# Seven block products whose banks alternate, and a new instruction order from the second token group on

## The chip, the core and the metric

The kernel runs on one core of one Trainium2 chip. The metric is the device time of one execution in microseconds (us): the median of three runs of the kernel before is 733.15 us (731.96 to 734.58).

Engine names as in the profile: PE is TensorE's matmul stream, PEld its weight loads, DVE VectorE, ACT ScalarE, POOL GpSimd, SP SyncE (which issues most of the DMAs). Each engine works through its own list of instructions in order and waits where an operand is not ready.

## The reference

An attention over 768 tokens of four sequences (eight heads of 64), with a local window and block summaries, feeds a gated feed-forward layer over all 3072 tokens:

```python
k_sum = k.reshape(B, H, nb, 32, D).max(axis=3)
v_sum = v.reshape(B, H, nb, 32, D).mean(axis=3)
scores_l = scale * q @ k.T            # kept where |i - j| < 16
scores_s = scale * q @ k_sum.T + log(32)
a = softmax(concat([scores_l, scores_s]))
attn = a @ concat([v, v_sum])
...
x = attn as (3072, 512)
xn = x / sqrt(mean(x * x) + 1e-6) * rms_g
g, val = xn @ w_gate, xn @ w_val      # 512 -> 1536
out = (silu(g) * val) @ w_out         # 1536 -> 512
```

Every product is made of 16-bit halves: a value is split into a high and a low part, and three matmuls (high by high, high by low, low by high) stand for one.

## The kernel before

**Units and groups.** Attention is done in 24 units of 128 tokens. For unit u: `prep_k` and `prep_q` scale, split and transpose (by a DMA) keys and queries, `scores u g` makes the scores of four heads, `expo u g` the exponentials, which a DMA transposes into `eT`, `attend u` multiplies them with the values that `prep_v` has put into `v1`, `v2h` and `v2l`, and `norm_a`, `norm_b` normalise the result and transpose it by a DMA into the group's `xT`. `v2h` exists once for all units: `prep_v` of the next unit writes half of it on ACT (L757), a DMA issued by POOL (L758) copies that half to the other partitions, and neither may start before the last `attend` that reads the old content.

The feed-forward layer takes the tokens in nine groups (384, 128, 256, then six of 384). Groups 0 to 4 use `gate_val grp f` (L1177: 12 matmuls for the gate, 12 for the value of 128 features, one PSUM bank each, two banks of the name `gv` in turn; then a tanh on ACT at L1181, two DVE operations at L1182 and L1184, and the split into `hh` on ACT and `hl` on DVE). `project grp f` (L1207) multiplies `hh` and `hl` with the output weights, three matmuls for each 128 tokens.

**Seven products.** Half the features of group 5 and all of groups 6 to 8 use a scheme with seven block products in place of eight. `make_t` prepares sums of the weights, `make_s grp c` (POOL, ACT, DVE) sums of the tokens, `seven grp f2` the seven products of two times 256 features, and `swish` what follows. A product is 12 matmuls of 192 columns (L1113). `seven` has two PSUM banks. Called X and Y here (Z is the bank of Y, used before it), they are filled in the program in this order, where X accumulates over four products and is copied out by ACT after each:

| product | X1 | Z2 | X3 | Y4 | X5 | X6 | Y7 |
|---|---|---|---|---|---|---|---|
| read out by | ACT L1135 | DVE L1138 | ACT L1140 | with X5 | ACT L1144, then DVE L1145 adds Y | ACT L1147 | DVE L1149 |

A product into a bank that is being read out waits for the reader.

**Who sets the order.** `PLAN` is a list of 764 steps in the order in which the program is recorded. `ORDER` then gives, engine by engine, a permutation of the recorded instructions (as jumps and run lengths), and `in_order` chains each engine's instructions to it. So products of one `seven` stand between matmuls of `project`, `scores` and `attend`, and may be exchanged where the data allow it.

Of the kernel before, what the change touches and what calls it, by code (L numbers as in the profile page):

```python
# [82 lines left out]
project 2 1 256 512; conv_o 0; sum_fold 2 0 0 2; gate_val 2 3 256; fill_k 10; expo 7 1; sum_load 2 0 0 3;
scores 8 0; project 2 2 256 512; scores 8 1; gate_val 2 4 256; sum_fold 2 0 0 3; project 2 3 256 512; conv_o 1;
prep_q 9; expo 8 0; gate_val 2 5 256; sum_load 2 0 1 0; attend 7; fill_k 11; project 2 4 256 512; prep_v 8;
gate_val 2 6 256; sum_load 2 0 1 1; load_unit 11; project 2 5 256 512; conv_o 2; expo 8 1; gate_val 2 7 256;
attend 8; gate_val 2 8 256; norm_a 7; project 2 6 256 512; sum_fold 2 0 1 0; sum_fold 2 0 1 1;
project 2 7 256 512; conv_o 3; gate_val 2 9 256; norm_b 7; scores 9 0; sum_load 2 0 1 2; prep_v 9;
gate_val 2 10 256; sum_fold 2 0 1 2; scores 9 1; norm_a 8; project 2 8 256 512; sum_load 2 0 1 3; norm_b 8;
project 2 9 256 512; conv_o 4; sum_fold 2 0 1 3; load_ks 2; gate_val 2 11 256; prep_q 10; expo 9 0;  # L90
sum_scale 2 0; project 2 10 256 512; gate_val 3 0 384; sum_load 2 1 0 0; gate_val 3 1 384; sum_fold 2 1 0 0;
sum_load 2 1 0 1; project 2 11 256 512; conv_o 5; expo 9 1; gate_val 3 2 384; scores 10 0; sum_fold 2 1 0 1;
split_ks 2; sum_load 2 1 0 2; load_k 12; project 3 0 384 768; sum_fold 2 1 0 2; gate_val 3 3 384;
sum_load 2 1 0 3; expo 10 0; attend 9; prep_k 12; project 3 1 384 768; prep_v 10; gate_val 3 4 384;
sum_fold 2 1 0 3; load_k 13; scores 10 1; sum_load 2 1 1 0; prep_k 13; fill_k 12; norm_a 9; expo 10 1;
project 3 2 384 768; project 3 3 384 768; norm_b 9; gate_val 3 5 384; sum_load 2 1 1 1; prep_q 11;
sum_fold 2 1 1 0; sum_fold 2 1 1 1; load_k 15; prep_k 14; fill_k 13; gate_val 3 6 384; sum_load 2 1 1 2;
sum_fold 2 1 1 2; project 3 4 384 768; load_k 16; sum_load 2 1 1 3; scores 11 0; project 3 5 384 768;
gate_val 3 7 384; expo 11 0; sum_fold 2 1 1 3; load_unit 12; load_unit 13; sum_load 3 0 0 0; attend 10;
prep_v 11; scores 11 1; gate_val 3 8 384; norm_a 10; prep_q 12; project 3 6 384 768; sum_scale 2 1; norm_b 10;  # L100
sum_load 3 0 0 1; expo 11 1; gate_val 3 9 384; prep_k 15; fill_k 14; project 3 7 384 768; attend 11; load_k 17;
prep_v 12; gate_val 3 10 384; load_unit 14; norm_a 11; prep_q 13; project 3 8 384 768; sum_fold 3 0 0 0;
sum_fold 3 0 0 1; sum_load 3 0 0 2; norm_b 11; prep_q 14; project 3 9 384 768; load_unit 15; sum_fold 3 0 0 2;
scores 12 0; scores 12 1; gate_val 3 11 384; expo 12 0; project 3 10 384 768; sum_load 3 0 0 3;
gate_val 4 0 384; prep_k 16; fill_k 15; sum_fold 3 0 0 3; expo 12 1; load_k 18; sum_load 3 0 1 0;
gate_val 4 1 384; make_t 0; make_t 1; load_unit 16; scores 13 0; project 3 11 384 768; sum_load 3 0 1 1;
gate_val 4 2 384; project 4 0 384 1152; project 4 1 384 1152; scores 13 1; gate_val 4 3 384; make_t 2;
make_t 3; expo 13 0; attend 12; project 4 2 384 1152; prep_k 17; fill_k 16; gate_val 4 4 384; prep_v 13;
expo 13 1; project 4 3 384 1152; gate_val 4 5 384; make_t 4; make_t 5; norm_a 12; prep_q 15; scores 14 0;
attend 13; project 4 4 384 1152; gate_val 4 6 384; norm_b 12; load_unit 17; expo 14 0; prep_v 14;  # L110
gate_val 4 7 384; project 4 5 384 1152; scores 14 1; norm_a 13; gate_val 4 8 384; sum_fold 3 0 1 0;
sum_fold 3 0 1 1; expo 14 1; sum_load 3 0 1 2; fill_k 17; project 4 6 384 1152; sum_fold 3 0 1 2;
gate_val 4 9 384; prep_q 16; norm_b 13; sum_load 3 0 1 3; project 4 7 384 1152; attend 14; scores 15 0;
sum_fold 3 0 1 3; load_ks 3; gate_val 4 10 384; sum_load 3 1 0 0; prep_v 15; project 4 8 384 1152;
sum_load 3 1 0 1; norm_a 14; sum_scale 3 0; sum_fold 3 1 0 0; sum_fold 3 1 0 1; expo 15 0;
project 4 9 384 1152; split_ks 3; scores 15 1; sum_load 3 1 0 2; gate_val 4 11 384; norm_b 14; load_k 19;
project 4 10 384 1152; sum_fold 3 1 0 2; sum_load 3 1 0 3; prep_k 18; sum_fold 3 1 0 3; project 4 11 384 1152;
prep_q 17; load_k 20; expo 15 1; gate_val 5 6 384; sum_load 3 1 1 0; prep_k 19; fill_k 18; gate_val 5 7 384;
make_t 6; make_t 7; load_k 21; sum_fold 3 1 1 0; project 5 6 384 1536; gate_val 5 8 384; scores 16 0;
attend 15; project 5 7 384 1536; sum_load 3 1 1 1; gate_val 5 9 384; make_t 8; expo 16 0; sum_fold 3 1 1 1;  # L120
scores 16 1; sum_load 3 1 1 2; prep_v 16; gate_val 5 10 384; sum_fold 3 1 1 2; norm_a 15; project 5 8 384 1536;
expo 16 1; norm_b 15; prep_k 20; fill_k 19; gate_val 5 11 384; make_s 5 0; make_s 5 1; make_t 9;
sum_load 3 1 1 3; scores 17 0; seven 5 0; sum_fold 3 1 1 3; load_unit 18; load_unit 19; project 5 9 384 1536;
load_k 22; sum_scale 3 1; attend 16; expo 17 0; prep_v 17; project 5 10 384 1536; norm_a 16; prep_q 18;
norm_b 16; seven 5 1; swish 5 0 1; load_unit 20; project 5 11 384 1536; make_t 10; swish 5 0 0; scores 17 1;
project 5 0 384 1536; expo 17 1; project 5 1 384 1536; make_t 11; swish 5 1 1; seven 5 2; swish 5 1 0;
scores 18 0; prep_k 21; fill_k 20; load_k 23; attend 17; expo 18 0; prep_v 18; norm_a 17; prep_q 19; norm_b 17;
swish 5 2 1; project 5 2 384 1536; prep_q 20; swish 5 2 0; load_unit 21; make_s 6 0; scores 18 1;
project 5 3 384 1536; make_s 6 1; seven 6 0; project 5 4 384 1536; project 5 5 384 1536; expo 18 1; prep_k 22;
fill_k 21; load_unit 22; swish 6 0 1; seven 6 1; swish 6 0 0; scores 19 0; expo 19 0; attend 18;  # L130
project 6 0 384 1920; prep_v 19; project 6 1 384 1920; swish 6 1 1; seven 6 2; swish 6 1 0; norm_a 18;
prep_q 21; norm_b 18; swish 6 2 1; project 6 2 384 1920; swish 6 2 0; seven 6 3; scores 19 1;
project 6 3 384 1920; expo 19 1; project 6 4 384 1920; prep_k 23; fill_k 22; scores 20 0; load_unit 23;
attend 19; swish 6 3 1; expo 20 0; seven 6 4; prep_v 20; project 6 5 384 1920; swish 6 3 0; norm_a 19;
scores 20 1; prep_q 22; project 6 6 384 1920; expo 20 1; fill_k 23; norm_b 19; swish 6 4 1; swish 6 4 0;
scores 21 0; seven 6 5; project 6 7 384 1920; attend 20; project 6 8 384 1920; prep_v 21; norm_a 20; prep_q 23;
norm_b 20; expo 21 0; project 6 9 384 1920; swish 6 5 1; swish 6 5 0; scores 21 1; make_s 7 0; make_s 7 1;
seven 7 0; project 6 10 384 1920; project 6 11 384 1920; expo 21 1; swish 7 0 1; seven 7 1; swish 7 0 0;
scores 22 0; project 7 0 384 2304; attend 21; expo 22 0; swish 7 1 1; seven 7 2; project 7 1 384 2304;
swish 7 1 0; prep_v 22; scores 22 1; project 7 2 384 2304; project 7 3 384 2304; swish 7 2 1; seven 7 3;  # L140
expo 22 1; norm_a 21; norm_b 21; swish 7 2 0; scores 23 0; attend 22; expo 23 0; seven 7 4; swish 7 3 1;
prep_v 23; swish 7 3 0; norm_a 22; scores 23 1; project 7 4 384 2304; norm_b 22; project 7 5 384 2304;
# [1115 lines left out]
```

## Time and profile before

| | |
|---|---|
| median of three runs | 733.15 us (731.96 to 734.58) |
| profiled execution, its own time | 731.4 us |
| its span, first to last instruction | 729.4 us |
| PE busy | 684.8 us, 94% of the span, 5846 matmuls |
| DVE busy | 587.9 us, 81% |
| ACT busy | 478.1 us, 66% |
| POOL busy | 314.5 us, 43% |
| granted TensorE clock, mean | 0.992 |

A matmul's duration in the trace is longer than the distance to the next one, because they are pipelined: work is read from start to start. Idle time in square brackets is the time that an engine stood still before a row, and the name behind it what ended that.

### The profile page before, as it was taken

Reading aid. Unit: us, or ns where it says so; the run is one execution under the profiler, and the core shown is the slowest. Engines: PE = TensorE matmul, PEld = TensorE weight load, DVE = VectorE, ACT = ScalarE, POOL = GpSimd, SP = SyncE. Lnnn points to the kernel's source line nnn. Section 1 sums busy time; section 2 is a strip of 40 time slices with the busy share of each in tenths; the row PEclk is TensorE's granted clock in tenths of the full one; section 3 lists DMA queues with packets and bytes.
Section 4 is the critical chain, followed back from the end, with each engine's and each line's share of the span. In section 5 each row is a group of like instructions: output and inputs, shape, how many; then the busy total and the mean of one; then the engine's idle time right before and its main releaser. Section 6 shows DMA issues by size and latency. Waiting matters only on the chain.

```text
span 729.4 us, 16150 instructions
## 1 busy us (share of the span) xinstructions
PE 684.8 (94%) x5846; PEld 495.2 (68%) x5846; DVE 587.9 (81%) x1594; ACT 478.1 (66%) x1023; POOL 314.5 (43%) x421
## 2 busy tenths in 40 slices
...
GB/s 196 310 306 247 204 98 112 112 112 125 153 153 139 117 106 184 178 141 172 131 110 133 114 182 113 123 148 117 91 106 118 113 91 71 48 53 44 2 1 44
DMA packets 243860, 93.33 MB, mean 128 GB/s; under 512 B 227716, under 2 KB 227716, under 8 KB 243780
## 3 DMA queue, kind: packets, MB, share of 16 engines
...
q0 software_dynamic: 1152, 1.22, 0.7%
q8 instruction: 46, 0.75, 0.5%
...
## 4 chain that ended last, share of the span: by engine, by line
PE 50%; DVE 16%; DMA 11%; ACT 9%; issue 6%; POOL 5%; SPq 1%; ACTq 0%; DVEq 0%; POOLq 0%
PE gv L1113 14%; PE acc L1207 14%; PE gv L1177 13%; ACT sm L791 2%; DMA eT<-ee 2%; PE att L948 2%; PE att L817 2%; DVE hl L372 2%; DMA hn<-in_v_dram 1%; PE att L776 1%; DVE sm L780 1%; DMA hn<-in_k_dram 1%; DVE w L474 1%; DVE v2l L759 1%; DVE th L1184 1%
## 5 line engine op out<-in xcount | busy, mean ns | idle before, releaser
L1177 PE MATMUL gv<-xT,w_gv 128*128 128x384 f16 (+2 forms) x1584 | 228.7, 299 | 10.9 <-DVE th L1182 9.3
L1177 PEld LDWEIGHTS <-w_gv 128*128 128x128 f16 x1584 | 141.5, 98 | 89.5 <-issue 22.6
L1207 PE MATMUL acc<-wo,hh 128*128 128x512 f16 (+1 forms) x576 | 178.0, 391 | 1.0 <-ACT hh L1164 0.7
L372 POOL TENSOR_TENSOR ee<-sm,ee 128x512 f16<-128x512 f32 (+1 forms) x72 | 72.2, 1018 | 104.0 <-ACT ee L367 99.4
L1207 PE MATMUL acc<-wo,hl 128*128 128x512 f16 (+1 forms) x288 | 110.8, 385 | 5.3 <-DVE hl L372 4.5
L1113 PEld LDWEIGHTS <-w_gv 128*128 128x128 f16 x1008 | 84.3, 98 | 11.5 <-issue 5.0
L791 ACT ACTIVATE sm<-sm,mx,c 128x192 f32<-128x192 f32 x144 | 68.9, 537 | 14.1 <-DVE mx L783 13.3
L1207 PEld LDWEIGHTS <-hh 128*128 128x128 f16 x432 | 39.8, 98 | 31.3 <-ACT hh L1164 1.1
L1181 ACT ACTIVATE th<-gv,gains 128x384 f32<-128x384 f32 (+2 forms) x66 | 33.9, 514 | 27.6 <-PE gv L1177 21.9
L1113 PE MATMUL gv<-S,w_gv 128*128 128x192 f16 x504 | 48.4, 246 | 3.0 <-ACT R L1144 1.9
L1113 PEld LDWEIGHTS <-wo 128*128 128x128 f16 x540 | 45.4, 98 | 5.7 <-issue 2.1
L372 DVE TENSOR_TENSOR hl<-th,hh 128x384 f16<-128x384 f32 (+3 forms) x66 | 44.0, 671 | 5.7 <-ACT hh L367 5.4
L780 DVE CUSTOM_DVE_ANT_0 sm<-att,mask 128x192 f32<-128x192 f32 x144 | 45.1, 349 | 3.2 <-PE att L776 1.7
L1113 PE MATMUL gv<-xT,w_gv 128*128 128x192 f16 x504 | 47.3, 246 | 0.3 <-ACT R L1147 0.3
L367 ACT CAST hh<-th 128x384 f16<-128x384 f32 (+3 forms) x66 | 29.3, 447 | 22.7 <-DVE th L1184 15.1
L1182 DVE SCALAR_TENSOR_TENSOR th<-th,gv 128x384 f32<-128x384 f32 (+2 forms) x66 | 31.2, 473 | 12.9 <-ACT th L1181 12.6
L1207 PEld LDWEIGHTS <-hl 128*128 128x128 f16 x216 | 21.1, 98 | 29.7 <-DVE hl L372 2.9
L618 ACT ACTIVATE junk<-hn 96x512 uint8<-96x512 f32 x48 | 30.0, 626 | 13.4 <-DMA hn<-in_v_dram 9.2
L367 ACT CAST ee<-sm 128x512 f16<-128x512 f32 (+1 forms) x72 | 34.2, 508 | 2.8 <-DMA eT<-ee 1.9
L758 POOL DMA_DIRECT2D v2h<-v2h x36 | 19.7, 548 | 36.9 <-ACT v2h L757 35.5
L1010 POOL TENSOR_TENSOR x_r<-x_r,consts 128x1 f32<-128x1 f32 x24 | 17.3, 721 | 42.0 <-DVE x_r L1009 41.5
L1113 PE MATMUL gv<-xT,wo 128*128 128x192 f16 x360 | 34.8, 246 | 0.5 <-DVE xT L1101 0.5
...
## 6 DMA issues: line engine op xcount, KB each, us to landing
...
```

Source lines behind the costliest of these rows:

```text
L367: nc.scalar.copy(o, i)
L372: (nc.vector if ENG.get(op, "p") == "v" else nc.gpsimd).tensor_tensor(o, a, b, op=ALU.subtract)
L618: nc.scalar.activation(junk[0:96], y[:, o:o + DM], AF.Square, accum_out=d["ss"][:, j:j + 1])
L758: {"s": nc.sync, "a": nc.scalar, "p": nc.gpsimd}[ENG.get("v2q", "a")].dma_start(v2h[other, r], v2h[rs, r])
L780: nc.vector.tensor_tensor_reduce(sm[:, i, :], pt[:, j * SC:(j + 1) * SC], mask, 1.0, NEG, op0=ALU.add, op1=ALU.max, accum_out=mx[:, i:i + 1])
L791: nc.scalar.activation(sm[:, i, :], sm[:, i, :], AF.Exp, scale=s["c"][:, 0:1], bias=mx[:, i:i + 1])
L1010: nc.gpsimd.tensor_tensor(r, r, nhalf, op=ALU.pow)
L1113: nc.tensor.matmul(bank[:, i * T2:(i + 1) * T2], lhsT=right(n, wi, c), rhs=left(xi, c), start=start, stop=(i == 1 and c == 1 and wi == 1), ...
L1177: nc.tensor.matmul(pt[:, 0:T], lhsT=w_gv[:, f - f % 2 + i, wi, c, f % 2, :], rhs=x[:, xi, c, 0:T], start=(n == 0), stop=(n == 3 * NC - 1))
L1181: nc.scalar.activation(th[:, 0:T], pg[:, 0:T], AF.Tanh, scale=f_sc[:, f - f % 2:f - f % 2 + 1])
L1182: nc.vector.scalar_tensor_tensor(th[:, 0:T], th[:, 0:T], 1.0, pg[:, 0:T], op0=ALU.add, op1=ALU.mult)
L1207: nc.tensor.matmul(accs[grp][j], lhsT=h[:, js], rhs=wo_hl[f // 2][:, wi, f % 2, :], start=(f == first and n == 0), stop=(f == (first - 1) ...
```

## The change

Two things change, and no instruction is added or removed: PE has 5846 matmuls in both.

First, in `seven`, Y4 and not X5 becomes the product that is copied out by ACT, X5 is added to it by DVE, and Y7 goes ahead of X6:

```diff
             product(Y, lambda xi, c: x[:, xi, c, up], tee(2), True)
+            nc.scalar.copy(r[1][:, :, 1], half(Y))
             product(X, ess(2), tee(0))
-            nc.scalar.copy(r[1][:, :, 1], half(X))
-            nc.vector.tensor_tensor(r[1][:, :, 1], r[1][:, :, 1], half(Y), op=ALU.add)
+            nc.vector.tensor_tensor(r[1][:, :, 1], r[1][:, :, 1], half(X), op=ALU.add)
+            product(Y, lambda xi, c: x[:, xi, 2 + c, up], tee(3))
+            nc.vector.tensor_tensor(r[0][:, :, 1], r[0][:, :, 1], half(Y), op=ALU.add)
             product(X, ess(1), block(1, 1))
             nc.scalar.copy(r[1][:, :, 0], half(X))
-            product(Y, lambda xi, c: x[:, xi, 2 + c, up], tee(3))
-            nc.vector.tensor_tensor(r[0][:, :, 1], r[0][:, :, 1], half(Y), op=ALU.add)
```

Second, `PLAN` from its 270th step on and `ORDER` of all five engines are new. PE's list is the same for its first 856 of 5701 recorded matmuls, which is up to 153.9 us of the trace of before. One line of each table:

```diff
-project 0 11 384 0; load_unit 9; load_unit 10; prep_k 10; fill_k 9; gate_val 2 0 256; project 1 10 128 384;
...
+gate_val 2 0 256; sum_load 2 0 0 2; project 2 0 256 512; gate_val 2 1 256; sum_fold 2 0 0 0; scores 7 1;
...
--39x12 27x3 -30x24 -124x10 246x9 -129x12 -138x18 120x45 259x3 -322x3 57x21 241x6 -247x12 24x3 211x3 -241x24 18 198x3
...
+-39x12 27x3 -30x24 -124x10 246x9 -129x12 -138x18 120x45 259x3 -322x3 57x21 244x3 -247x12 24x3 -27x12 217x3 -190 192x3
...
```

The new tables are four lines longer, so the code behind them has numbers higher by four in the lists of the kernel after (L791 is L795, L372 is L376). In `seven` the line numbers after are L1139 (copy of X1), L1144 (X3), L1147 (Y4), L1149 (adds X5), L1151 (adds Y7) and L1153 (copy of X6).

ACT, at the products of `seven 6 0` and the start of `seven 6 1` (`gv_7469` is X of `seven 6 0` before; after, `gv_7478` is its X, `gv_7519` its Y and `gv_7611` the X of `seven 6 1`). Before:

```order
L791 ACTIVATE sm_7429<-sm_7429,mx_7430,c_6912 128x192 x3
L1140 COPY R_7467<-gv_7469 128x2x192
L367 CAST ee_7590<-sm_7429 128x2x2x64
L1217 DMA out_0_dram<-ob_7587 128x512
L367 CAST ee_7590<-sm_7429 128x4x128
L1144 COPY R_7468<-gv_7469 128x2x192
L733 ACTIVATE qs_7392<-qr_l_7030,q_s_7384 128x8x64
L1147 COPY R_7468<-gv_7469 128x2x192
```

After:

```order
L1147 COPY R_7477<-gv_7519 128x2x192
L795 ACTIVATE sm_7414<-sm_7414,mx_7415,c_6924 128x192 x2
L1144 COPY R_7476<-gv_7478 128x2x192
L1221 DMA out_0_dram<-ob_7575 128x512
L371 CAST ee_7598<-sm_7414 128x2x2x64
L1221 DMA out_0_dram<-ob_7581 128x512
L371 CAST ee_7598<-sm_7414 128x4x128
L737 ACTIVATE qs_7407<-qr_l_7074,q_s_7399 128x8x64
L1139 COPY R_7609<-gv_7611 128x2x192
L1153 COPY R_7477<-gv_7478 128x2x192
```

Before, three copies in a row read the same bank X; now the copies of Y, X, the next `seven`'s X, and X follow each other.

ACT, at `prep_v 8` (L757 writes the two halves of `v2h` for unit 8, L761 its `v1`; L1181 is a gate's tanh, L791 the exponentials of `expo 8 1`, L592 the weights of `conv_o`). Before:

```order
L757 ACTIVATE v2h_142<-v2r_l_2689,kv1_s_2160 64x4x64
L1181 ACTIVATE th_3387<-gv_3361,gains_129 128x256
L761 ACTIVATE v1h_140<-vr_l_2688,kv1_s_2160 128x8x64
L757 ACTIVATE v2h_142<-v2r_l_2689,kv1_s_2160 64x4x64
L791 ACTIVATE sm_3154<-sm_3154,mx_3155,c_2836 128x192 x4
```

After:

```order
L761 ACTIVATE v2h_142<-v2r_l_2689,kv1_s_2160 64x4x64
L596 ACTIVATE wo1_3380<-cv_3376,scales_2135 128x512
L596 ACTIVATE wo1_3380<-cv_3378,scales_2135 128x512
L761 ACTIVATE v2h_142<-v2r_l_2689,kv1_s_2160 64x4x64
L1185 ACTIVATE th_3282<-gv_3256,gains_129 128x256
L371 CAST hh_3252<-th_3248 128x256
L765 ACTIVATE v1h_140<-vr_l_2688,kv1_s_2160 128x8x64
```

The second half of `v2h` now stands ahead of `v1h`, a tanh and a split of `gate_val`, where it stood behind them.

POOL, at the normalisation of unit 17, the last of group 6 (L1010 is `norm_a`, `xs` the split of `norm_b` that the transposing DMA into `xT` waits for, `ee` the splits of `expo 18 0`). Before:

```order
L758 DMA v2h_142<-v2h_142 64x264 x2
L1010 TENSOR_TENSOR x_r_7336<-x_r_7336,consts_86 128x1
L372 TENSOR_TENSOR ee_7314<-sm_7236,ee_7314 128x2x128
L372 TENSOR_TENSOR xs_7359<-x_7263,xs_7359 128x512
L372 TENSOR_TENSOR ee_7314<-sm_7236,ee_7314 128x4x128
```

After:

```order
L762 DMA v2h_142<-v2h_142 64x264 x2
L1014 TENSOR_TENSOR x_r_7336<-x_r_7336,consts_86 128x1
L376 TENSOR_TENSOR xs_7340<-x_7263,xs_7340 128x512
L376 TENSOR_TENSOR ee_7322<-sm_7244,ee_7322 128x2x128
L376 TENSOR_TENSOR ee_7322<-sm_7244,ee_7322 128x4x128
```

`xs` of unit 17 moved ahead of both splits of the exponentials.

## Rows read from the trace of the kernel before

**Rows 1.** Stages: stretch, length, busy PE, PEld, DVE, ACT, POOL, PE clock, DMA.

```profile
201.60:264.70 63.10, 57.77 (x518) 47.11 (x517) 53.18 (x152) 44.91 (x105) 29.74 (x32) 0.97 0.75 131
...
462.10:655.20 193.10, 186.83 (x1972) 149.82 (x1970) 155.36 (x443) 133.74 (x294) 83.75 (x103) 1.00 0.54 97
```

**Rows 2.** Waits of PE from 201 us on: who for whom, total us, times, longest.

```profile
PE gv L1177 <- DVE th L1182: 4.3, 5, 1.1
PE att L817 <- DMA v2h<-v2h: 2.0, 1, 2.0
PE gv L1113 <- ACT R L1144: 1.9, 3, 0.7
PE att L817 <- DMA eT<-ee: 1.4, 2, 1.2
PE gv L1113 <- ACT R L1140: 1.1, 2, 0.6
PE gv L1177 <- DVE th L1184: 1.0, 1, 1.0
```

**Rows 3.** Timeline of PE at X5, X6, Y7 of seven 6 0, and at X5, X6 of 8 0.

```profile
514.52 1.15 PE L1113 MATMUL gv<-S,w_gv 128*128 128x192 f16 x12 [0.57 <-ACT R L1140]
516.24 1.15 PE L1113 MATMUL gv<-S,w_gv 128*128 128x192 f16 x12 [0.57 <-ACT R L1144]
517.23 1.15 PE L1113 MATMUL gv<-xT,wo 128*128 128x192 f16 x12
...
663.13 1.15 PE L1113 MATMUL gv<-S,w_gv 128*128 128x192 f16 x12
665.00 1.15 PE L1113 MATMUL gv<-S,w_gv 128*128 128x192 f16 x12 [0.72 <-ACT R L1144]
```

**Rows 4.** Timeline around attend 7 and attend 8, all engines.

```profile
234.76 0.19 PE L817 MATMUL att<-v2h,eT 128*128 128x65 f16 x1
...
234.79 4.09 PE L1177 MATMUL gv<-xT,w_gv 128*128 128x256 f16 x36
...
236.48 0.52 POOL L758 DMA_DIRECT2D v2h<-v2h  x1 [3.20 <-ACT v2h L757]
...
241.88 0.20 PE L817 MATMUL att<-v2h,eT 128*128 128x65 f16 x1 [2.01 <-DMA v2h<-v2h]
```

**Rows 5.** Stretches of 2 us behind that wait, columns as in rows 1.

```profile
242.00:244.00 2.00, 2.00 (x17) 1.65 (x16) 1.42 (x2) 0.49 (x2) 2.00 (x3) 0.80 0.63 105
244.00:246.00 2.00, 2.00 (x11) 1.51 (x10) 0.82 (x2) 1.62 (x5) 1.96 (x2) 0.50 1.65 147
246.00:248.00 2.00, 2.00 (x12) 1.49 (x11) 1.74 (x3) 0.46 (x2) 0.00 (x0) 0.85 0.27 55
```

**Rows 6.** Timeline of PE, ACT, POOL between attend 17 and Y4 of seven 6 0.

```profile
496.92 0.60 PE L1207 MATMUL acc<-wo,hh 128*128 128x512 f16 x2 [0.65 <-ACT hh L1164]
...
497.82 0.62 ACT L367 CAST xs<-x 128x512 f16<-128x512 f32 x1
...
498.31 0.39 PE L1207 MATMUL acc<-wo,hl 128*128 128x512 f16 x1 [0.78 <-DVE hl L1165]
...
498.51 1.16 POOL L372 TENSOR_TENSOR xs<-x,xs 128x512 f16<-128x512 f32 x1
...
511.55 0.82 PE L1113 MATMUL gv<-xT,wo 128*128 128x192 f16 x8 [0.51 <-DVE xT L1101]
```

**Rows 7.** Timeline at project 1 6: DVE, POOL and PE.

```profile
178.21 3.92 DVE L666 SCALAR_TENSOR_TENSOR khl<-kr_l,kv_s,khl 128x512 f16<-128x512 f32 x1
...
178.38 0.74 POOL L1074 TENSOR_TENSOR S<-S 128x256 f32<-128x256 f32 x1
...
179.07 2.50 POOL L585 TENSOR_TENSOR cv<-wo 128x512 f32<-128x512 f32 x2
...
182.38 0.50 PE L1207 MATMUL acc<-wo,hl 128*128 128x512 f32 x1 [2.48 <-DVE hl L372]
```

**Rows 8.** The same DVE line at prep_k 7, undisturbed.

```profile
146.65 0.75 DVE L666 SCALAR_TENSOR_TENSOR khl<-kr,kv_s,khl 128x512 f16<-128x512 f32 x1
```

More of the change, by code (lines that the diff above doesn't have):

```diff
@@ L83 @@
[L83 to L142, printed above, removed]
@@ new lines @@
+make_s 5 0; make_s 5 1; sum_load 3 1 1 3; fill_k 19; expo 16 1; make_t 9; load_k 22; norm_b 15;
+sum_fold 3 1 1 3; load_unit 18; load_unit 19; project 5 9 384 1536; seven 5 0; sum_scale 3 1; attend 16;
+expo 17 0; project 5 10 384 1536; make_t 10; prep_v 17; norm_a 16; prep_q 18; seven 5 1; project 5 11 384 1536;
+swish 5 0 1; swish 5 0 0; scores 17 1; norm_b 16; load_unit 20; project 5 0 384 1536; expo 17 1;
+project 5 1 384 1536; make_t 11; seven 5 2; swish 5 1 1; swish 5 1 0; prep_k 21; fill_k 20; scores 18 0;
@@ new lines @@
+swish 6 2 0; scores 19 1; project 6 2 384 1920; expo 19 1; project 6 3 384 1920; scores 20 0; prep_k 23;
+fill_k 22; load_unit 23; attend 19; project 6 4 384 1920; swish 6 3 1; expo 20 0; project 6 5 384 1920;
+swish 6 3 0; seven 6 4; prep_v 20; scores 20 1; norm_a 19; prep_q 22; fill_k 23; expo 20 1; norm_b 19;
+swish 6 4 1; project 6 6 384 1920; swish 6 4 0; scores 21 0; seven 6 5; project 6 7 384 1920; attend 20;
+expo 21 0; prep_v 21; norm_a 20; prep_q 23; norm_b 20; project 6 8 384 1920; swish 6 5 1; swish 6 5 0;
```

244 lines of the change are left out of this document (149 added, 95 removed).

## The prediction

> **What bounds the kernel.** I read the page first, then the waits of PE, then stretches of the span, then the timeline at the places that these name. The page shows PE busy for 684.8 of 729.4 us, 94%, and the other engines between 43% and 81%, so a gain can come only from time in which PE stands still or runs at a lower clock. The stretches [rows 1] show where that is: between 201.6 and 264.7 us PE is idle for 63.10 - 57.77 = 5.3 us, at a mean granted clock of 0.97; between 462.1 and 655.2 us, where the seven products are, for 193.10 - 186.83 = 6.3 us. PE's list is the same up to 153.9 us, so what happens before is out of reach.
>
> The waits from 201 us on [rows 2] are short. The reader is to see three kinds there: the gate's PSUM bank (L1177 waits for L1182 or L1184), the transfers of attention (`v2h`, `eT`), and the banks of `seven` (L1113 waits for the copies L1140 and L1144). The six rows come to 11.7 us. A dozen others in that list are under one microsecond each.
>
> **The change part by part.** The same instructions are executed before and after, so the sum has only waits and clock in it.
>
> *a. The banks of seven.* In `seven 6 0`, X5 follows X3 and X6 follows X5 directly. Both stand still, 0.57 us each [rows 3], because ACT must first have read X. The step from X5's start to X6's is 516.24 - 514.52 = 1.72 us; the next, to another bank, is 517.23 - 516.24 = 0.99. One such meeting costs 1.72 - 0.99 = 0.73 us, in `seven 8 0` 665.00 - 663.13 - 0.99 = 0.88. There are five of them in `seven 6 0`, `7 0` and `8 0`, two at L1140 and three at L1144 [rows 2], so the cost is about 4 x 0.73 + 0.88 = 3.8 us. In the new order a product of the other bank, 0.99 us, stands between X3 and X5 and one between X5 and X6. A reader that is ready 0.73 us after the product has then 0.26 us to spare. That is little: the order of ACT after has two exponentials between the copies of Y4 and X3. I take 3.3 us; the bounds are 0 (each wait comes back as a late reader) and 3.8.
>
> *b. Attend 8.* Its first matmul waits 2.01 us for the transfer of `v2h` [rows 4]. The last matmul of `attend 7` starts at 234.76; ACT writes the two halves, POOL issues the second transfer at 236.48, having stood still 3.20 us for ACT, and PE goes on at 241.88. The chain is 241.88 - 234.76 = 7.1 us long. Before, PE has three blocks of 12 `gate_val` matmuls (4.09 us) and one `project` block in that time. In the new order it has four blocks of `gate_val` (4 x 4.09 / 3 = 5.5 us) and six of `project`, three matmuls each; two take 0.60 us [rows 6], so six blocks are 3.6 to 5.4 us. That makes 9 to 11 us over a chain of 7.1, and on ACT the second half of `v2h` now stands ahead of the tanh and of `v1h`, which shortens the chain too. Behind the wait the granted clock is 0.80, 0.50 and 0.85 in three stretches of 2 us in which PE is busy all the time [rows 5]; 0.50 is the level of 1.2 GHz. That costs 2 x (0.20 + 0.50 + 0.15) = 1.7 us more. I take both, 2.0 + 1.7 = 3.7; the bounds are 0 and 3.7.
>
> *c. The bank of gate_val's value.* One wait for L1184, 1.0 us [rows 2], stands in `gate_val 2 3`. Between the two uses of that bank the order has one block before (4.09 / 3 = 1.4 us) and over two after. I take 1.0 (0 to 1.0).
>
> *d. Project 1 6.* PE waits 2.48 us for `hl` at 182.38 [rows 7]. DVE was late there, since L666 took 3.92 us where the same line takes 0.75 undisturbed [rows 8]. Beside it POOL ran 0.74 and 2.50 us: 0.75 + 0.74 + 2.50 = 3.99, so DVE seems to have stood for the whole of both. In the new order there are some three more microseconds of PE's work between `gate_val 1 6` and `project 1 6`. I take 2.5 (0 to 2.5).
>
> *e. Unit 17.* `project 5 2` waits 0.65 and 0.78 us for the split of its `swish`, and Y4 of `seven 6 0` 0.51 us for `xT` of group 6 [rows 6], 1.9 in all. The new order puts two more products and a block of `project` (0.99 x 2 + 0.6 = 2.6 us) ahead of `project 5 2` and about one more ahead of Y4. POOL's move by itself is worth nearly nothing: the high half of `xs` is ready at 497.82 + 0.62 = 498.44, and POOL starts on `xs` at 498.51. I take 1.2 (0 to 1.9).
>
> *f. Given back.* The other waits are drawn anew. Of the rows above, L1182 (4.3) and `eT` (1.4) stay, and the short waits that no row shows are about as much again: some 10 us. They could vanish or double. In the order I count fewer tight places than before (a gate's bank that comes back after under 2 us of PE's work: some 11, before some 16), but PE arrives earlier at each operand by all that a to e save, and DVE, busy for 53.18 of 63.10 us between 201.6 and 264.7 [rows 1], does not become faster by it. I count 4 us as lost again (between -5 and +10). In the tail two blocks of `project` fewer than before lie between the last product and the first use of its `hh`; I put that inside the 4.
>
> The sum is 3.3 + 3.7 + 1.0 + 2.5 + 1.2 - 4 = 7.7 us. It is made against the profiled execution, 731.4 us, which lies 1.75 below the median of the runs: 731.4 - 7.7 = 723.7, and 725.4 as a median.
>
> On part d the Trainium skill, page "SBUF — State Buffer", section "🔬 SBUF: two separate sides", says that the port pair which DVE and GpSimd share is an exclusive lock held for a whole instruction, the other engine standing blocked. The trace agrees at L666 (3.92 against 0.75 us beside POOL). By that rule the 2.5 us are no saving of this place, but move to wherever DVE next meets POOL; the sum would then be 5.2.
>
> **The rivals.**
>
> *Slower: POOL's work meets DVE's at worse places.* All lists are new, POOL's too, and it still runs the same weight and attention work between 154 and 470 us. A clash of the kind in rows 7 costs DVE 3.92 - 0.75 = 3.2 us. Where a split or a gate that PE needs within 2 us stands behind it on DVE, nearly all of that reaches PE, as 2.48 of 3.2 did, and it may take the clock down as in rows 5 (1.7). The sum before anything is given back is 11.7, so the change turns slower from five such new clashes on: six cost 6 x 2.5 = 15 and, with one fall of the clock, 16.7, so the time is 733.15 - 11.7 + 16.7 = 738. Against it: from 201 us on, the longest wait in the list is 2.0 us, so clashes that reach PE are rare in the old order. The rule named under d would raise the chance of this case.
>
> *No change: attention sets the pace.* If waits at `gate_val` only stand in for work that attention needs anyway (unit for unit, scores, exponentials, transfer, `attend`), PE loses at later L1182 or `eT` waits what it gains at a to e, and the time is 731 to 735. For it: `v2h` exists once, and its chain of 7.1 us recurs with every unit. Against it: only one `attend` of the sixteen after 201 us waits 2 us for it, and in the order after the banks of `seven` are late in the kernel, where attention has little left to do.
>
> *More: nothing is given back.* If the new order removes the old waits and the L1182 ones become no more, the sum is 11.7 and the time 721; with half of the rest gone too, 717.
>
> *The banks alternate, yet the waits stay.* If ACT comes more than 0.26 us late to each of the copies (its exponentials stand ahead of them), part a gives nothing and the time is 728.7. That lies inside the forecast's own range.
>
> **How the numbers follow.** A measurement of this kernel can tell about 0.3%, 2.2 us. The forecast, with a part of the gain given back (720 to 730), has 0.50; more has 0.18 (714 to 720); no change has 0.16, of which 0.02 is faster, 0.13 the same and 0.01 slower; slower has 0.16. That makes 0.70 faster, 0.13 the same, 0.17 slower. The range leaves out 0.04 at the fast end, below 715, and the outer part of the slower case, above 737.
>
> **What would show it.** In the profile after, X5 and X6 of `seven 6 0` start 0.99 us after the product before them with no wait for L1144 or L1149; `attend 8` has no `v2h` wait and the stretches behind it a clock of 1.00; PE's wait for `hl` at `project 1 6` is gone; PE's idle time between 201 us and the end falls by about 6 us. The prediction is wrong if waits for L1182 or for a DMA exceed 10 us from 201 us on, or if DVE instructions of several times their usual length stand ahead of PE's waits.

## The result, and the profile after

The changed kernel takes 726.0 us (median of 4 runs, 723.25 to 727.86) where the kernel before takes 733.0 beside it (731.96 to 734.58): a ratio of 0.990, with a 95% interval of 0.986 to 0.994. The forecast was 725.4. The profiled execution has a span of 721.5 us after 729.4, and is the fastest of the four.

PE's busy time falls by 1.2 us (684.8 to 683.6), so 6.7 of the 7.9 us of span are standing time. The page's line on PE, and PE's waits from 201 us on (in us: total, times, longest), as in [rows 2]; the list's remaining rows are 0.2 us each:

```profile
PE 683.6 (95%) x5846; PEld 495.6 (69%) x5846; DVE 582.4 (81%) x1594; ACT 474.6 (66%) x1023; POOL 316.2 (44%) x421
```

```profile
PE gv L1181 <- DVE th L1186: 4.0, 7, 1.1
PE att L821 <- DMA eT<-ee: 3.6, 4, 1.6
PE att L780 <- DVE hl L1169: 2.6, 1, 2.6
PE att L780 <- DMA qT<-qs: 0.9, 2, 0.5
PE gv L1117 <- DVE S L1105: 0.6, 2, 0.4
```

With line numbers lower by four these are the kinds of [rows 2]. The wait for `v2h`, both for the banks of `seven` and the one for L1184 are gone. The gate's bank is as before (4.0 after 4.3), `eT` has grown from 1.4 to 3.6, and one wait for `hl`, at `scores 18 1`, from 0.6 to 2.6. All rows together are 12.3 us after 16.5; from 154 us on, where the two orders begin to differ, 18.5 after 23.8. The profile of before also has the fall of the clock of [rows 5], 1.7 us, and the one after has none from 154 us on.

The last products of `seven 6 0` and the first of `seven 6 1` in PE's timeline (Y7, X5, X1 of the next, X6, then X3 of the next), with no wait in brackets any more:

```profile
509.33 1.15 PE L1117 MATMUL gv<-xT,wo 128*128 128x192 f16 x12
510.32 1.15 PE L1117 MATMUL gv<-S,w_gv 128*128 128x192 f16 x12
511.31 1.15 PE L1117 MATMUL gv<-xT,w_gv 128*128 128x192 f16 x12
512.30 1.15 PE L1117 MATMUL gv<-S,w_gv 128*128 128x192 f16 x12
513.29 1.15 PE L1117 MATMUL gv<-S,wo 128*128 128x192 f16 x12
```

Each starts 0.99 us after the one before, where two steps took 1.72 and more [rows 3].

Stages by PE's work tell where the time went better than the clock on the wall does. The table takes the start of the first matmul of each step from PE's timeline and gives the length of the stretch to the next (us). The steps that stand between differ between the two orders, above all in the last three rows: of the work that lies between `seven 5 0` and `seven 6 0` before, the changed order has two blocks of `project` and eight matmuls of `scores` (0.65 us a block and 0.33 us for four: 2.0 us) ahead of `seven 5 0`, and two blocks (1.3 us) behind the start of `seven 6 0`.

| stretch, from first matmul to first matmul | before | after |
|---|---|---|
| start to gate_val 1 0 (the same list) | 131.4 | 131.8 |
| gate_val 1 0 to gate_val 1 6 | 42.2 | 45.1 |
| gate_val 1 6 to gate_val 2 0 | 28.1 | 23.9 |
| gate_val 2 0 to gate_val 2 6 | 29.1 | 29.2 |
| gate_val 2 6 to gate_val 3 0 | 34.0 | 30.0 |
| gate_val 3 0 to seven 5 0 | 197.4 | 198.2 |
| seven 5 0 to seven 6 0 | 40.6 | 37.5 |
| seven 6 0 to the end | 226.7 | 225.7 |

The 3.1 us of the row `seven 5 0` to `seven 6 0` are therefore moved work and no gain, while the last row is 1.0 us shorter with 1.3 us more to do. One profile gives a row only roughly. In the kernels below that keep a row's lists, those of before take 42.1 to 42.7 us from gate_val 1 0 to 1 6, 31.3 to 32.4 from gate_val 2 6 to 3 0 (34.0 above holds the fall of the clock), 197.4 to 200.4 from gate_val 3 0 on and 226.4 to 227.3 in the last row; the changed ones 45.1 to 45.6, 30.0 to 32.3, 198.2 to 201.0 and 225.3 to 225.7.

### The profile page after: what moved, and what is told of

It is laid out like the page before. It is cut to its first block, busy times and chain, and to the rows that moved or that the text cites. A ratio compares the mean times of both kernels' runs of the same rounds, so it can differ in the third digit from the quotient of the medians.

```text
span 721.5 us, 16197 instructions
## 1 busy us (share of the span) xinstructions
PE 683.6 (95%) x5846; PEld 495.6 (69%) x5846; DVE 582.4 (81%) x1594; ACT 474.6 (66%) x1023; POOL 316.2 (44%) x421
## 4 chain that ended last, share of the span: by engine, by line
PE 48%; DVE 23%; DMA 9%; ACT 8%; issue 5%; POOL 3%; SPq 2%; DVEq 0%; ACTq 0%; POOLq 0%
PE gv L1117 13%; PE acc L1211 13%; PE gv L1181 12%; DMA eT<-ee 3%; ACT sm L795 2%; DMA hn<-in_v_dram 2%; DVE sm L784 2%; PE att L952 2%; PE att L821 2%; DVE S L1072 2%; DVE th L1188 2%; DVE th L1186 2%; DVE v2l L763 1%; SPq L691 1%; PE att L780 1%
## 5 line engine op out<-in xcount | busy, mean ns | idle before, releaser
L1181 PE MATMUL gv<-xT,w_gv 128*128 128x384 f16 (+2 forms) x1584 | 229.0, 298 | 10.8 <-DVE th L1186 10.3
L1181 PEld LDWEIGHTS <-w_gv 128*128 128x128 f16 x1584 | 140.9, 98 | 90.8 <-issue 24.7
L376 POOL TENSOR_TENSOR ee<-sm,ee 128x256 f16<-128x256 f32 (+1 forms) x72 | 71.3, 1009 | 80.9 <-ACT ee L371 62.3
L795 ACT ACTIVATE sm<-sm,mx,c 128x192 f32<-128x192 f32 x144 | 69.9, 538 | 27.9 <-DVE mx L787 25.5
L376 DVE TENSOR_TENSOR hl<-th,hh 128x384 f16<-128x384 f32 (+3 forms) x66 | 39.7, 603 | 7.3 <-ACT hh L371 7.1
L1166 DVE SCALAR_TENSOR_TENSOR att<-att,R 128x384 f32<-128x384 f32 x42 | 23.3, 561 | 22.7 <-ACT att L1165 22.7
L1211 PEld LDWEIGHTS <-hl 128*128 128x128 f16 x216 | 21.1, 98 | 27.5 <-DVE hl L1169 2.0
L1186 DVE SCALAR_TENSOR_TENSOR th<-th,gv 128x384 f32<-128x384 f32 (+2 forms) x66 | 31.2, 473 | 7.8 <-ACT th L1185 7.4
L780 PE MATMUL att<-kT,qT 128*128 128x192 f16 x288 | 33.4, 246 | 3.9 <-DVE hl L1169 2.6
L628 POOL TENSOR_TENSOR hn<-hn 96x512 f32<-96x512 f32 x18 | 25.7, 1430 | 24.9 <-DMA hn<-in_v_dram 19.5
```

The source lines that it names most:

```text
L376: (nc.vector if ENG.get(op, "p") == "v" else nc.gpsimd).tensor_tensor(o, a, b, op=ALU.subtract)
L628: eng.tensor_tensor(x[:, 0:w], x[:, 0:w], y[:, 0:w], op=op)
L780: nc.tensor.matmul(pt[:, j * SC:(j + 1) * SC], lhsT=s["qT"][:, a * H + h, :], rhs=kT[:, h, :], start=(a == 0), stop=(a == 1))
L795: nc.scalar.activation(sm[:, i, :], sm[:, i, :], AF.Exp, scale=s["c"][:, 0:1], bias=mx[:, i:i + 1])
L1181: nc.tensor.matmul(pt[:, 0:T], lhsT=w_gv[:, f - f % 2 + i, wi, c, f % 2, :], rhs=x[:, xi, c, 0:T], start=(n == 0), stop=(n == 3 * NC - 1))
L1186: nc.vector.scalar_tensor_tensor(th[:, 0:T], th[:, 0:T], 1.0, pg[:, 0:T], op0=ALU.add, op1=ALU.mult)
```

## The experiments

Kernels whose label begins with b are the kernel before with one part changed; those with a are the changed kernel. The tables of numbers are edited so that the lists of instructions change as shown; a part of the code changes only where it is said. Each ratio is against the kernel before, run on the same chip, with its 95% interval. A place in the lists is named by step and number; `X1'` is X1 of the next `seven`.

| label | median us | ratio to before | interval |
|---|---|---|---|
| b_seven | 737.3 | 1.0056 | 1.0031 to 1.0082 |
| b_seven2 | 742.3 | 1.0118 | 1.0096 to 1.0140 |
| b_seven3 | 733.8 | 0.9992 | 0.9964 to 1.0019 |
| b_attend8 | 732.1 | 0.9988 | 0.9966 to 1.0009 |
| b_hl | 732.2 | 0.9986 | 0.9964 to 1.0008 |
| b_hl_gate | 731.3 | 0.9972 | 0.9948 to 0.9997 |
| b_pool | 729.9 | 0.9955 | 0.9934 to 0.9976 |
| b_pool_attend8 | 728.7 | 0.9941 | 0.9913 to 0.9969 |
| a_qs | 726.2 | 0.9907 | 0.9878 to 0.9935 |
| a_qs_pool | 728.0 | 0.9920 | 0.9894 to 0.9945 |
| a_early | 723.4 | 0.9859 | 0.9823 to 0.9896 |
| a_early2 | 725.6 | 0.9878 | 0.9852 to 0.9905 |

### Part a alone, three times

b_seven: the new code in `seven 6 0`, `7 0` and `8 0` only, and there:

```diff
 PE:  Y4 X3
-     X5 X6 Y7 X1'
+     Y7 X5 X1' X6
 ACT:
+     copy of Y4
      (one exponential) copy of X3
-     copy of X5 (prep_q) copy of X6, copy of X1'
+     (prep_q) copy of X1', copy of X6
 DVE:
-     add Y4, prep_q 20, add Y7
+     add Y7, prep_q 20, add X5
```

> The kernel before with part a alone: in seven 6 0, 7 0 and 8 0 the new code (Y4 copied by ACT, X5 added by DVE, Y7 ahead of X6), and on PE the order Y4 X3 Y7 X5, X1 of the next seven, X6. Everything else stays in the order of before. If the same-bank waits are a real cost on PE's path (my theory), the waits of L1113 for the copies (3.0 us of idle time in seven 6 0, 7 0, 8 0) vanish, X5 and X6 start 0.99 us after the product ahead of them, and the time falls by 3 to 3.8 us, to about 0.995. If PE only gets earlier to the next wait (rival), the steps are 0.99 us too, but the time falls by under 1 us and the waits for swish or xT grow. If ACT is late (second rival), L1113 waits for the copy of Y4 or X3 instead and nothing is gained.

It became slower by 4 us. The five waits for the copies of X3 and X5 went, but a reader on DVE took their place, and X's next user waits three times for the copy of X6 (1.1 us in all). DVE and PE of b_seven at X5, X1' and X6 (here L1114 is the product, L1147 the add of X5, L370 and L735 `prep_q 20`):

```profile
517.11 1.15 PE L1114 MATMUL gv<-xT,w_gv 128*128 128x192 f16 x12
517.45 0.77 DVE L370 COPY qs<-qs 128x512 f16<-128x512 f16 x1 [0.50 <-ACT qs L734]
518.13 0.74 DVE L735 SCALAR_TENSOR_TENSOR qs<-qr_l,q_s,qs 128x512 f16<-128x512 f32 x1
518.91 0.29 DVE L370 COPY qs<-qs 128x512 f16<-128x512 f16 x1
519.12 0.55 DVE L1147 TENSOR_TENSOR R<-R,gv 128x384 f32<-128x384 f32 x1
519.72 0.49 PE L1114 MATMUL gv<-S,w_gv 128*128 128x192 f16 x4 [1.46 <-DVE R L1147]
```

X5 is complete about 517 us, but its add waits behind three operations of `prep_q`; X6 should have started at 518.1 and stands still 1.46 us. This is the late reader that the prediction named under a, only on DVE instead of ACT.

b_seven2 mended that order:

```diff
 DVE:
-     add Y7, prep_q, add X5, swish, add Z2'
+     add Y7, add X5, prep_q, add Z2', swish
 PE:
-     X6 (scores) Z2' X3'
+     X6 X3' (scores) Z2'
```

(In `seven 7 1` and `8 1` Y4 and X5 moved with them, so that no two products of one bank meet.)

> Part a again on the kernel before, this time with the readers in step: on DVE the adds of Y7 and X5 follow each other ahead of the copies of qs, the add of the next seven's Z2 stands ahead of swish, and on PE X3 of the next seven stands ahead of its Z2. In the run without these moves X6 waited 1.46 us for the add of X5 that stood behind prep_q on DVE, and the time rose by 4 us. If that was only the readers' order, the waits of L1113's banks around seven 6 0, 7 0 and 8 0 now sum to under 0.6 us and the stretch from X1 of seven 6 0 to the end is 3 us shorter than before (226.6 us in the trace of before), some 0.996 in time. If the new product order itself costs (banks that come back after one product of 0.99 us whatever the readers do), waits of 2 us or more remain and the time is at best that of before.

Slower still, by 9 us. The waits of b_seven2 from 500 us on:

```profile
PE att L777 <- DVE hl L1176: 3.9, 3, 3.0
PE gv L1114 <- ACT R L1141: 3.2, 1, 3.2
PE att L777 <- DVE mx L781: 2.4, 1, 2.4
```

No add of X5 is among them. But on DVE the add of Z2', which I had put ahead of `swish`, now stood for its product, which I had put behind `scores`:

```profile
521.58 0.55 DVE L1139 TENSOR_TENSOR R<-R,gv 128x384 f32<-128x384 f32 x1 [2.46 <-PE gv L1114]
```

Behind it stood `swish` and what the next `scores` wait for (2.4 us at 523.86); and on ACT the split of that `swish` stood ahead of the copy of X3', for which X5' waits. b_seven3 therefore let the other `swish`, whose sums are ready first, go first:

```diff
 PLAN:
-swish 6 0 1; seven 6 1; swish 6 0 0
+swish 6 0 0; seven 6 1; swish 6 0 1
 ACT:
-     copy of X1', copy of X6, tanh and split of swish 6 0 1, copy of X3'
+     tanh of swish 6 0 0, copy of X1', split of swish 6 0 0, copy of X6, copy of X3', tanh of swish 6 0 1
 DVE:
-add Z2', swish 6 0 1, swish 6 0 0
+swish 6 0 0, add Z2', swish 6 0 1
```

> Part a once more on the kernel before. In the two runs ahead the waits for the banks went, but the swish that needs X6, now the last product, still stood first on ACT and DVE, and what was queued behind it made PE wait 2.4 to 3.2 us at scores and X5. Here the two swish steps of seven 6 0, 7 0 and 8 0 change places (the one whose sums are ready first goes first), and the copy of the next seven's X3 stands ahead of the second. If the product order is good once all lists of readers follow it, the stretch from X1 of seven 6 0 to the end is 2.5 to 3.5 us shorter than before's 226.6, and the time about 0.996. If it costs by itself, the stretch is not shorter than 226.6.

The time is that of before (0.9992), and X1 of `seven 6 0` to the end takes 227.4 us where before has 226.7. The two longest sums of waits of b_seven3 from 500 us on:

```profile
PE gv L1114 <- ACT R L1151: 1.7, 3, 0.7
PE att L818 <- DVE mx L781: 1.0, 1, 1.0
```

Three waits for the copy of X6 (L1151) remain. ACT of b_seven3 shows why: the split of `swish` (L1175) that I had put ahead of it stood 1.60 us for DVE.

```profile
521.14 0.48 ACT L1175 CAST hh<-att 128x384 f16<-128x384 f32 x1 [1.60 <-DVE att L1174]
521.52 0.48 ACT L1151 COPY R<-gv 128x384 f32<-128x384 f32 x1
```

So all three of my versions lost what the alternating banks gave: with these lists of ACT and DVE the product order does not pay. In the changed kernel the waits are gone; that the order pays there, and what it is worth, is not shown, since it was not taken out of the change.

### Part b alone

```diff
 PE:
-     attend 8 (first 10 matmuls)
      gate_val 2 8 (24 matmuls)
+     attend 8 (first 10 matmuls)
```

> The kernel before with part b alone: on PE the first ten matmuls of attend 8 stand behind the 24 matmuls of gate_val 2 8 instead of ahead of them. By my theory the wait of 2.0 us for v2h goes, the granted clock behind it stays at 1.00, and the time falls by 3 to 3.7 us (0.995 to 0.996), less some 0.4 us if gate_val 2 8 now waits for a bank. By the rival (attention sets the pace) PE waits as long within the next units, for L1182 or a transfer, and the time is within 1 us of before. If the clock falls anyway, the fall does not come from this wait, and only 2 us are gained.

The wait for `v2h` is gone; PE waits 0.57 us at `gate_val` right after, as expected. `gate_val 2 6` to `gate_val 3 0` takes 30.9 us. The comparison is not the 34.0 of before, though: b_hl has the same wait, and the clock does not fall behind it. PE and stretches of 2 us of b_hl there (columns as in [rows 1]):

```profile
241.56 0.20 PE L817 MATMUL att<-v2h,eT 128*128 128x65 f16 x1 [1.98 <-DMA v2h<-v2h]
```

```profile
241.00:243.00 2.00, 1.44 (x14) 1.30 (x15) 2.00 (x2) 0.46 (x1) 2.00 (x3) 1.00 0.75 150
243.00:245.00 2.00, 2.00 (x17) 1.75 (x16) 1.52 (x5) 1.85 (x5) 2.00 (x2) 1.00 1.14 148
```

There the stretch takes 32.4 us, in b_seven 32.1. Six kernels below and above that keep this place as it was (b_seven, its two successors, b_hl, b_hl_gate, b_pool) have a wait of 0.9 to 2.0 us there, no fall behind it, and 31.3 to 32.4 us. So the wait costs about 1 us (0.4 to 1.5), and the 1.7 us of [rows 5] belonged to one execution of seven. On the whole time 1 us is too little to be told from nothing.

### Part d alone

b_hl and b_hl_gate move DVE's work, b_pool moves POOL's:

```diff
 DVE (b_hl):
+L372 TENSOR_TENSOR hl<-th,hh
 L666 SCALAR_TENSOR_TENSOR khl<-kr_l,kv_s,khl
-L372 TENSOR_TENSOR hl<-th,hh
 DVE (b_hl_gate): as b_hl, and
+L1182 L1184 of gate_val 1 7
 L666 SCALAR_TENSOR_TENSOR khl<-kr_l,kv_s,khl
-L1182 L1184 of gate_val 1 7
 POOL (b_pool):
+L372 ee x2, L372 xs
 L1074 TENSOR_TENSOR S<-S
 L585 TENSOR_TENSOR cv<-wo x2
-L372 ee x2, L372 xs
```

> The kernel before with one move on DVE: hl of gate_val 1 6 stands ahead of L666 of prep_k 9, which took 3.92 us beside POOL. By part d of the sum the wait of 2.48 us at project 1 6 goes and the time falls by 2.5 us. By the rival (the clash only moves) L666 still takes some 3.9 us, the L1182 of gate_val 1 7 behind it on DVE is as late as before, PE then waits there for the gate's bank for about 2 us, and the time falls by 0 to 0.5 us.

> As the run before, but the two DVE operations of gate_val 1 7 stand ahead of L666 as well. If DVE's standing still beside POOL is the cause and only what is queued behind it suffers, this takes 2 to 2.5 us off the time, where the run before takes 0 to 0.5; L666 is short (0.75 us) if it now starts after POOL's two instructions, and some 2 to 3 us if it starts beside them. If the pace is set elsewhere, the time stays within 1 us of before and other waits of PE grow.

> The kernel before with one move on POOL: the last product of make_t 1 and the two of conv_o 1 (0.74 and 2.50 us, which stood beside L666 or, moved ahead, beside hl) come after the split of norm_b 5, some 14 us later. If the shared use of DVE's and POOL's side of memory is the cause, L666 and hl take 0.75 and 0.28 us, the wait at project 1 6 goes (-2.5 us), and whatever two-operand DVE instruction meets the moved POOL work instead (prep_q 8's at 195.8) grows to 2 us or more: the stretch from gate_val 1 6 to gate_val 2 0 (28.1 us) is 1.5 to 2.5 us shorter. If L666 was slow for another reason, it or hl stays over 2 us.

Neither move on DVE did what either theory expected. Timeline of b_hl (POOL, DVE, PE):

```profile
178.51 0.74 POOL L1074 TENSOR_TENSOR S<-S 128x256 f32<-128x256 f32 x1
178.53 3.32 DVE L372 TENSOR_TENSOR hl<-th,hh 128x128 fp32r<-128x128 f32 x1
179.19 2.50 POOL L585 TENSOR_TENSOR cv<-wo 128x512 f32<-128x512 f32 x2
...
181.78 0.74 DVE L666 SCALAR_TENSOR_TENSOR khl<-kr_l,kv_s,khl 128x512 f16<-128x512 f32 x1
181.91 0.49 PE L1207 MATMUL acc<-wo,hl 128*128 128x512 f32 x1 [1.89 <-DVE hl L372]
```

Now `hl` itself takes 3.32 us, and L666, behind it and after POOL is done, 0.74. Which DVE instruction is slow is decided by POOL, not by the instruction. b_hl is not told apart from before. In b_hl_gate `hl` also takes 3.32 us; its interval ends just under 1, and its stretch (28.9 us) holds a fall of the clock, so that a gain of some 1 us beside it can be neither shown nor excluded.

In b_pool the two are as long as they are without company, and the wait at `project 1 6` is gone. DVE of b_pool there:

```profile
180.79 0.75 DVE L666 SCALAR_TENSOR_TENSOR khl<-kr_l,kv_s,khl 128x512 f16<-128x512 f32 x1
181.46 0.28 DVE L372 TENSOR_TENSOR hl<-th,hh 128x128 fp32r<-128x128 f32 x1
```

`gate_val 1 6` to `gate_val 2 0` takes 25.9 us after 28.1, the operation of `prep_q 8` that the moved work meets takes 1.05 instead of 0.75 (2 or more were expected), and the time falls by 3 us (0.9955). The Trainium skill, page "SBUF — State Buffer", section "🔬 SBUF: two separate sides", gives the rule behind it, an exclusive lock of the port pair that DVE and GpSimd share. The trace agrees, 3.32 against 0.28 us for the same `hl`; here three POOL instructions in a row held DVE out to the end of the last.

### Two parts together

The edits of b_pool and b_attend8 in one kernel.

> Two of the moves on the kernel before together: POOL's three products some 14 us later, and the first ten matmuls of attend 8 behind gate_val 2 8. Alone they took 2.2 us off the stretch from gate_val 1 6 to gate_val 2 0 and 1.3 us off the one from gate_val 2 6 to gate_val 3 0. If gains add up, the two stretches are 25.9 and 30.9 us and the time is 0.993 to 0.996; if PE only comes earlier to the next wait, the second stretch is back at 32 us, since it begins 2 us earlier against attention's chain, and the time is that of POOL's move alone (0.9955).

The two stretches are 25.8 and 30.9 us, as each alone, and the ratio is 0.9941. In these two stretches the gains add up; in the whole time the interval overlaps that of b_pool. By the medians these two moves, on POOL and PE, give 4 us where the whole change gives 7; that the change has its gain at the same places is not shown by it.

### The longest wait of the changed kernel

Timeline of the changed kernel at `scores 18 1`, where PE waited 0.62 us before:

```profile
497.81 1.78 POOL L1096 TENSOR_TENSOR R<-xT 128x768 f32<-128x768 f16 x1 [1.14 <-DMA xT<-xs]
498.00 1.93 DVE L373 COPY qs<-qs 128x512 f16<-128x512 f16 x2
499.86 0.61 DVE L1167 SCALAR_TENSOR_TENSOR att<-att,scales,R 128x384 f32<-128x384 f32 x1
...
501.51 0.55 DVE L1169 TENSOR_TENSOR hl<-att,hh 128x384 f16<-128x384 f32 x1
502.11 0.33 PE L780 MATMUL att<-kT,qT 128*128 128x192 f16 x2 [2.60 <-DVE hl L1169]
```

The two copies of `qs` take 1.93 us; of 36 such copies the median is 0.286 and the longest, here, 1.733. `swish` stands behind them. a_qs moves them; a_qs_pool moves POOL's work too:

```diff
 DVE (a_qs):
-L738 qs, L373 qs x2
 L1167 L1166 L1167 (swish 5 2), L1169 hl, L784, L1169 hl
+L738 qs, L373 qs x2
 POOL (a_qs_pool): as a_qs, and
-L1096 R<-xT x2
+L1096 R<-xT
 L1099 L1100 (make_s 6 0)
+L1096 R<-xT
```

> The changed kernel with one move on DVE: the three operations on qs of prep_q 19, of which the copies took 1.73 us beside POOL's 1.78, stand behind the splits of swish 5 2, for which PE waited 2.60 us at scores 18 1. By the theory that a clash delays whatever is queued behind it, that wait shrinks to under 0.5 us; PE then comes to seven 6 0 earlier than its sums S, which hang on POOL, so about 1.5 us of it are lost again there: 0.5 to 1.5 us faster than the changed kernel. If nothing is lost again, 2.3 us.

> As the run before, and on POOL the second and third operation of make_s 6 0 stand ahead of make_s 6 1's first, so that S of seven 6 0 is ready some 1.5 us earlier. If POOL's order decides what is lost again, this run keeps 2 us or more of the 2.6, and is about 722 to 724 us where the changed kernel has 726; if not, it equals the run before.

The wait at `scores 18 1` went to 0.06 us in both, and nothing was gained: 0.9907 and 0.9920. Waits of a_qs from 494 us on:

```profile
PE gv L1117 <- DVE xT L1105: 1.7, 2, 0.9
PE gv L1117 <- ACT S L1104: 0.6, 1, 0.6
PE att L821 <- DMA eT<-ee: 0.5, 1, 0.5
PE gv L1117 <- DVE S L1105: 0.4, 1, 0.4
```

The sums for `seven 6 0` come when ACT, DVE and POOL have made them, so PE, 2.5 us earlier, waits for them four times. The theory that the order of POOL's work decides this was wrong: a_qs_pool has these waits too, 2.9 us in all. And the clock fell behind these waits. Stretches of a_qs:

```profile
508.00:510.00 2.00, 1.65 (x11) 1.35 (x11) 2.00 (x4) 2.00 (x5) 0.00 (x0) 0.64 0.00 0
510.00:512.00 2.00, 2.00 (x15) 1.84 (x13) 0.29 (x1) 1.46 (x5) 0.56 (x1) 0.51 0.32 121
```

That is 2 x (0.36 + 0.49) = 1.7 us more. In a_qs_pool three such stretches are at 0.50 and those beside them at 0.89 and 0.90, 3.4 us by the same sum.

### The early waits of the changed kernel

The stretch that became longer (45.1 us after 42.2) ends with a wait of 2.30 us. Ahead of it stand two of the four products of this line that POOL runs between 171 and 184 us in either kernel:

```profile
171.83 2.49 POOL L589 TENSOR_TENSOR cv<-wo 128x512 f32<-128x512 f32 x2
171.93 1.19 DVE L552 TENSOR_SCALAR cv<-cv 128x12 int32<-128x12 int32 x1
173.16 1.19 DVE L553 TENSOR_SCALAR cv<-cv 128x12 int32<-128x12 int32 x1
174.44 0.72 ACT L737 ACTIVATE qs<-qr,q_s 128x512 f16<-128x512 f32 x1 [2.44 <-DVE q_s L450]
176.95 0.83 PE L1181 MATMUL gv<-xT,w_gv 128*128 128x128 f16 x12 [2.30 <-DVE th L1186]
```

In the kernel before, the first of these two DVE operations has no POOL product beside it:

```profile
163.49 0.17 DVE L548 TENSOR_SCALAR cv<-cv 128x12 int32<-128x12 int32 x1
```

Here each lasts about as long as one POOL product; DVE comes late to `q_s`, ACT with it, and the tanh and L1186 of `gate_val 0 10` stand behind that. a_early moves them ahead, a_early2 has the last two lines besides (for gate_val 1 4, 0 10 and 1 6 the second operation, L1188, moves too):

```diff
 DVE:
+L1186 (gate_val 1 4) ahead of L670 (prep_k 8), L545 (scale_h)
+L1186 (gate_val 1 5) ahead of L766 (prep_v 6)
+L1186 (gate_val 0 10) ahead of L553 (scale_h)
 ACT:
+L1185 (gate_val 0 10) ahead of L737 (prep_q 6), L567
 a_early2, ACT:
+L1185 (gate_val 1 6) ahead of L567, L732, L761, L732
 a_early2, DVE:
+L1186 (gate_val 1 6) ahead of L738 (prep_q 6)
```

> The changed kernel with its new waits between gate_val 1 0 and gate_val 1 6 taken up (PE waited 1.6, 0.5 and 2.3 us there for L1186, behind work for scale_h and prep_v on DVE and behind a scaling of queries on ACT): the first DVE operations of gate_val 1 4, 1 5 and 0 10 and the tanh of gate_val 0 10 stand ahead of that work. If such waits are only a matter of what stands ahead, the stretch from gate_val 1 0 to gate_val 1 6 (45.1 us) is 3 us shorter, and the run to the start of gate_val 2 0 keeps 2 us or more of it: about 723 to 724 us. If the work between sets the pace, the stretch behind it grows by as much and the time stays at 726.

> As the run with the early gate operations on the changed kernel, and the next wait that this uncovered is taken up too: there PE waited 2.16 us at gate_val 1 7 for L1186 of gate_val 1 6, whose tanh stood on ACT behind a scaling, two sums of squares and v2h. Here the tanh, and on DVE L1186, stand ahead of these. If waits in this stretch are each their own, gate_val 1 0 to gate_val 2 0 (69.0 us in the changed kernel, 69.8 with the early operations) falls to 67.5 to 68 us and the time to 721 to 723 us. If DVE's work between sets the pace (DVE is busy for 40.4 of the 47.7 us from 153.9 on), the wait moves on once more and the stretch stays at 69 to 70.

In a_early the stretch is 42.3 us, 2.8 shorter, and the next one 27.5, 3.6 longer: PE waits 2.16 us at `gate_val 1 7` instead, and its clock falls. Stretches of a_early:

```profile
178.00:180.00 2.00, 1.73 (x15) 1.72 (x14) 1.81 (x6) 1.68 (x4) 0.65 (x3) 0.56 1.09 204
180.00:182.00 2.00, 2.00 (x7) 1.56 (x6) 1.82 (x4) 0.30 (x2) 1.98 (x3) 0.58 0.91 183
```

In a_early2 that wait is gone, and others stand in its place:

```profile
178.65 0.35 PE L577 MATMUL att<-cv,ones 128*128 128x1 f32 x2 [1.08 <-DVE cv L575]
182.90 0.83 PE L780 MATMUL att<-kT,qT 128*128 128x192 f16 x8 [1.30 <-DMA qT<-qs]
```

`gate_val 1 0` to `gate_val 2 0` takes 69.0, 69.8 and 69.3 us in the changed kernel, a_early and a_early2, as if the work between set the pace there. It is not shown: the 69.8 hold the fall of the clock, some 1.7 us, a_qs and a_qs_pool with the changed kernel's lists take 69.6 and 69.8, and b_pool and b_pool_attend8 get through the same stretch in 68.5 and 68.0. Both a_early and a_early2 are clearly faster than the kernel before. The median of a_early, 723.4, is the lowest of all, but its interval overlaps that of the change, so whether it beats the change stays open.

## Why the prediction was right, and where it was not

The time was right to 0.6 us, and so was the sign. That closeness is in part luck: of the terms of the sum, a and f held in size, b and d were too large, and c and e came to nothing. The sum also counted a fall of the clock that the one profiled execution had and six others had not. And PE's waits from 201 us on fell by 4.2 us, where about 6 were forecast.

*a* (3.3 us): right in the changed kernel. The five waits, 3.0 us, are gone, 3.8 us by the prediction's count of steps; one step, to X5 of `seven 8 1`, has become 1.27 us, 0.28 too long, which leaves 3.5. That the time falls by as much is not shown; the last row of the table, 1.0 us shorter with 1.3 us more work, is what the trace has for it. That readers have little to spare was the right doubt, and its price was set too low: the prediction let a late reader cost what was gained, and b_seven and b_seven2 lost 4 and 9 us.

*b* (3.7): the wait is gone, but the term was mis-sized. The step that failed is "behind the wait the granted clock is 0.80, 0.50 and 0.85 ... I take both": the fall is not a property of that wait. The wait alone was worth about 1 us. The waits for `eT`, 2.2 us more than before, stand elsewhere but for 0.50 us at 246.16.

*c* (1.0): the wait moved to another product of the gate; L1186 has seven waits where L1182 had five.

*d* (2.5): right at its place, and right in its cause. The wait of 2.48 us is gone, and POOL's move alone gives 2.2 us of stretch. In the change the two stretches from `gate_val 1 0` to `gate_val 2 0` gain only 70.3 - 69.0 = 1.3 us, half of the term: two of POOL's products now clash with L552 and L553, and PE waits 2.30 us behind that; the two after them, at 180.58, meet L763 (2.61 us, median 0.48), which costs PE at most 0.20. This is what the prediction's other sum says, in which the clash moves to the next place where DVE meets POOL; how much of the missing 1.2 us it is, a_early does not settle.

*e* (1.2): wrong. The three waits (1.9) are gone, but the copies of `qs` now met POOL, and the wait at `scores 18 1` grew by 2.0 us.

*f* (4 given back): right in size. From 201 us on, a, b, c and e took 3.0 + 2.0 + 1.0 + 1.9 = 7.9 us of waits away, and the total fell by 16.5 - 12.3 = 4.2, so 3.7 came back. Counted from 154 us on, with d, it is 10.4 away, 5.3 less in total, and 5.1 back.

The slower rival's mechanism, a clash of DVE with POOL at a worse place, did appear, twice (2.30 and 2.60 us) and not five times. By the prediction's own sign, DVE instructions of several times their usual length ahead of PE's waits, this forecast would count as wrong, though the time came out: L373 took 1.73 us where the median is 0.29, L552 1.19 where before has 0.17. The change does not make such clashes rarer: from 131 us on, 36 DVE instructions before and 38 after last over 0.5 us longer than the median of their kind, 34.1 and 33.3 us in all; what counts is which of them PE waits behind. That PE only comes earlier to the next wait, as the rival without a change has it, was seen at `seven 6 0` (a_qs) and stays open from `gate_val 1 0` on (a_early); it does not hold everywhere, for the stretches that b_pool and b_attend8 shortened stayed short together.
